# One transfer per block of x for both partition halves, and v's second weight split placed ahead of a normalisation

## The chip, the core and the metric

The kernel runs on one core of a Trainium2 chip. A core has a TensorE (PE in the profile, with its weight loads shown as PEld), a VectorE (DVE), a ScalarE (ACT), a GpSimd (POOL) and a SyncE (SP). SP and POOL issue the transfers that this text is about, each from its own instruction queue; 16 DMA engines carry them out. The metric is the device time of one execution in microseconds (us), and the number compared is the median of several runs. The profile is one further execution, with its own time.

## The reference

```python
xn = _layernorm(x, axis=-1)                    # x: 1 x 2048 x 576
s  = attention(xn)                             # 32 heads of 18 columns, wqkv, softmax, wo
g  = _silu(((xn @ w_gate) * (xn @ w_up)) @ w_down)   # 4608 columns in between
return x + s * g
```

Everything is float32. The kernel keeps that precision by writing each operand as a high part in the matmul's own format and a low rest, and by adding the products high by high, low by high and high by low.

## The kernel before

**Setting up (the first 195 us).** The 2048 rows of x are taken in four chunks of 512 (`NCH`). Each chunk is normalised (`norm`), turned into columns by transposes (`to_columns`), and multiplied with the weights of q and k in nine blocks of 128 columns (`qk_block`). The results go to DRAM (`sqk`). The weights of v come in two halves: `v_fetch(h)` loads one, `v_split(h)` makes its high part on ACT (line 493) and its low part on POOL (line 494), five pieces each. `v_block` (line 502) multiplies a group of 128 rows with both halves, so the first `v_block`, right after chunk 1, needs `v_split(1)` done. The columns of chunks 1 to 3 go to DRAM too (`sx`, nine blocks for each chunk, by `x_store`).

**The main part (195 to about 2505 us).** TensorE is used as two halves of 64 rows each, r = 0 and r = 1. On the one half runs "up" of the gated unit, on the other "gate": both multiply with the same columns of x, so every block of x stands twice in the pair of tiles `xg`, in partitions 0 to 63 and again in 64 to 127. The loop over gated units goes chunk by chunk, 18 units in each (`units`, `NF2`). A unit has two pairs of 27 matmuls for each half (`gu_op`, line 753; three in a row use one block of x, blocks 0 to 8) and then its down product (`down_op`, line 804). Between these matmuls stand those of attention: scores for the row maximum (line 648), transposed scores for the softmax (line 700) and the product with v (line 711).

**How a new chunk of x comes in.** There are three changes of chunk. In a chunk's last unit, each half, when it has done its three matmuls with a block (`k % 3 == 2`), issues the transfer of that block of the next chunk into its own 64 partitions: r = 0 from SP's queue and r = 1 from POOL's (`x_block`, lines 461 to 468). Block 4 spans both tiles and takes two transfers. The waiting is done by the issuing queue: a transfer is held there until TensorE has read the old block.

**What sets the order.** The whole main part is an order written out before it runs: `order()` (line 1249) keeps a planner's clock for each half and each engine and picks the next instruction by due times. `there["x", c, b, r]` (lines 962 and 964) is the time at which the planner believes that a block has landed; a gated matmul of the new chunk is placed no earlier. `moved` (line 1017) is the planner's clock of the SP queue. Each engine then runs its own list strictly in that order.

Of the kernel before, what the change touches and what calls it, by code (L numbers as in the profile page):

```python
# [20 lines left out]
FT = mybir.dt.float32  # L21
# [20 lines left out]
def kernel(  # L42
# [10 lines left out]
    nc = tc.nc  # L53
# [20 lines left out]
    sx = dram.tile([NCH, 9, 64, 2, 512], FT, name="sx")  # L74
# [9 lines left out]
    def bank(tag, bufs, k=None):  # L84
        if tag == "g":
            if k is None:
                k = turns[0] = (turns[0] + 1) % 4
            return psum.tile([128, 512], FT, name="pg", tag=f"g{k}", bufs=1)
        return psum.tile([128, 512], FT, name="p" + tag, tag=tag, bufs=bufs)
# [78 lines left out]
    clk, free, split_at = [0.0, 0.0], {"DVE": 0.0, "ACT": 0.0, "POOL": 0.0}, {}  # L168
# [7 lines left out]
    def engine(eng, start, length):  # L176
        start = max(free[eng], start)
        free[eng] = start + max(length - HIDDEN[eng], 0.03)
        return start + length
# [150 lines left out]
    def load_x(c):  # L330
        xin[c] = ep.tile([128, 4, D], FT, name="xin", bufs=2)
        for t in range(4):
            nc.sync.dma_start(xin[c][:, t, :], x2[c * 512 + t * 128:c * 512 + t * 128 + 128, :])
# [28 lines left out]
    def norm(c, ts=range(4)):  # L362
        for t in ts:
            norm_stats(c, t)
        for t in ts:
            norm_apply(c, t)
# [73 lines left out]
    def qk_block(b, c):  # L440
        w, ninth = (t[:, b % 2] for t in wq[b // 2])
        p = bank("a" if nqk[0] % 2 else "b", 2)
        nqk[0] += 1
        for n, (a, e) in enumerate(QK_PAIRS):
            nc.tensor.matmul(p, w[:, a, :] if a < 9 else ninth, xcs[c][:, e, :], start=n == 0,  # L445
                             stop=n == len(QK_PAIRS) - 1)
        hl = pp.tile([128, 2, 512], FR, name="hl", bufs=3)
        nc.scalar.activation(hl[:, 0, :], p, AF.Copy)
        nc.vector.tensor_tensor(hl[:, 1, :], p, hl[:, 0, :].bitcast(FT), op=OP.subtract)
        g0 = blocks[b]  # L450
        for kind in range(2):
            lo, hi = max(g0, kind * D), min(g0 + 128, (kind + 1) * D)
            if lo < hi:
                dst = sqk[kind, :, lo - kind * D:hi - kind * D, c * 512:(c + 1) * 512]
                nc.sync.dma_start(dst.rearrange("h r s -> r h s"), hl[lo - g0:hi - g0].bitcast(FT))


    def x_part(b, part):
        return divmod(2 * b + part, 9)

    def x_block(c, b, r):
        queue = nc.gpsimd if r else nc.sync
        if b == 4:
            for part in range(2):
                queue.dma_start(xg[part][r:r + 64, 8 - 8 * part, :].bitcast(FT), sx[c, b, :, part, :])
        else:
            i, k = x_part(b, 0)
            queue.dma_start(xg[i][r:r + 64, k:k + 2, :].bitcast(FT), sx[c, b])

    vbox, vrows, vturn = {}, [], [0]  # L470

    def more_rows(pool, n):
        for _ in range(n):
            vrows.append(pool.tile([128, H, DH + 1], FT, name=f"vo{len(vrows)}"))
            nc.gpsimd.memset(vrows[-1], 1.0)
# [10 lines left out]
    def v_split(h):  # L486
        if h == 0:
            vbox["w"] = vp.tile([128, 10, D], FR, name="wv")
            more_rows(vp, 3)
        raw, wv = vbox["raw"], vbox["w"]  # L490
        cs = slice(h * HALF, (h + 1) * HALF)
        for k, d, lo in ((0, 0, 4), (1, 1, 5), (2, 2, 6), (3, 3, 7), (4, 8, 9)):
            nc.scalar.activation(wv[:, d, cs], raw[:, k, :], AF.Copy)
            nc.gpsimd.tensor_tensor(wv[:, lo, cs], raw[:, k, :], wv[:, d, cs].bitcast(FT),
                                    op=OP.subtract)
# [16 lines left out]
    def w_now(i):  # L512
        wq[i], todo = w_split(raws[i], 1 if i == 4 else 2, ep if i == 2 else pp if i == 4 else None)
        for f, a in todo:
            f(*a)

    def w_fetch(i):
        raws[i] = w_load([(wqkv, b) for b in blocks[2 * i:2 * i + 2]])
# [27 lines left out]
    for c in range(NCH):  # L546
        if c + 2 < NCH:
            load_x(c + 2)
        for b in range(3):
            qk_block(b, c)  # L550
            if c == 0 and b == 0:
                w_now(2)
        if c + 1 < NCH:
            to_columns(c + 1)
        for b in range(3, 6):
            qk_block(b, c)
            if b < 5 and c + 2 < NCH:
                norm(c + 2, (0, 1) if b == 3 else (2, 3))
            if c in (1, 2):
                x_store(c, range(3 * (b - 3), 3 * (b - 2)))  # L560
            if c < 2 and b == 3:
                v_split(c)
            if c == 0 and b == 5:
                v_fetch(1)
            if c == NCH - 1 and b == 3:
                w_now(3)
        if c == 1:
            w_fetch(3)
            for t in range(4):
                v_block(t)  # L570
            w_fetch(4)
        if c == 2:
            w_now(4)
# [21 lines left out]
    for t in range(8, NT):  # L595
# [4 lines left out]
        if t == 11:  # L600
            xg = [xcp.tile([128, 9, 512], FR, name="xc")]
# [28 lines left out]
    with ExitStack() as mid:  # L630
# [115 lines left out]
        def gu_start(r, n):  # L746
            ready(gdone, n)
            return bank("g", 1, slots[r, "g"])
# [45 lines left out]
        def alone(u, n):  # L794
            return u == len(units) - 1 and n == 7
# [148 lines left out]
            wos[1] = wpool.tile([128, 2, D], FR, name="wos2", tag="wgu", bufs=2)  # L944
            nc.sync.dma_start(wos[1].bitcast(FT), swo[:, 8:10, :])

        passed, xdone = {}, []

        def stream(r, kind):

            def glu(n):
                c, q = units[n // 2]
                box = []
                for k in range(len(TERMS)):
                    def work(k=k):
                        if k == 0:
                            box.append(gu_start(r, n))
                        gu_op(r, n, box[0], k)
                        if q == NF2 - 1 and n % 2 and k % 3 == 2 and c < NCH - 1:
                            x_block(c + 1, k // 3, 64 * r)  # L960
                            if r:
                                there["x", c + 1, k // 3, r] = engine("POOL", clk[r] + 0.5, 0.75 + 0.6 * (k == 14)) + 3.0
                            else:
                                there["x", c + 1, k // 3, r] = moved(clk[r] + 0.5, 0.285)
                        if n == 2 * len(units) - 1 and k == 13:
                            xdone.append(r)
                            if len(xdone) == 2:
                                wo_fetch()
                        if k == len(TERMS) - 1:
                            highs.append((gate_end if r else up_end)(n, box[0]))  # L970
                    end = (("DVE", 0.685) if r else ("ACT", 0.595)) if k == len(TERMS) - 1 else None
                    yield 0.231, k == 0, work, end, ("g", n, k), len(TERMS)

            def down(u, n):
                own = alone(u, n)
                key = u, n, r * own
                s, i = divmod(n, 2)
                for k in range(len(DTERMS)):
                    def work(k=k):
                        if (own or r == 0) and k == 0:  # L980
                            passed[key] = down_start(r, u)
                        down_op(r, u, s, i, passed[key], k, {"POOL": nc.gpsimd, "ACT": nc.scalar, "DVE": nc.vector}[soonest()])
                        if (own or r) and k == len(DTERMS) - 1:
                            acts.append(by_act(u, i, clk[r] + 0.33))
                            down_end(u, s, i, passed.pop(key), acts[-1])
                    end = None
                    if (own or r) and k == len(DTERMS) - 1:
                        end = (None, 0.0)
                    yield 0.132, (own or r == 0) and k == 0, work, end, ("d", u, 6 * n + k), len(DTERMS)

            if kind == "g":
                for n in range(2 * len(units)):
                    yield from glu(n)
            else:
                for u in range(len(units)):
                    for n in range(8):
                        yield from down(u, n)
# [19 lines left out]
        def moved(start, size):  # L1017

            queue[0] = max(queue[0], start) + size / 0.24
            return queue[0] + 2.0  # L1020

        due, jobs, rows_done = [], [], {}
        there, queue = {}, [0.0]
        na = nb = 0
        part_work = len(units) * (2 * 27 * 0.231 + 4 * 12 * 0.132)
        part = part_work + (TOTAL + N + LEAD) * 0.231
# [417 lines left out]
```

## Time and profile before

| what | value |
|---|---|
| median of 3 runs | 2612.92 us (2612.11 to 2613.13) |
| the profiled execution, its own time | 2611.95 us |
| its span, first to last instruction | 2610.2 us |
| granted TensorE clock, mean | 1.000 |
| moved by the DMA engines | 434.34 MB, 166 GB/s over the span |
| transfers of x blocks in the main part | 24 of 256 KB and 6 of 128 KB from SP, the same from POOL |

The page has the busy time of each engine, the span in 40 slices, the DMA queues, the chain of work that ended last, the costliest groups of instructions and the DMA issues. Beside it stand answers of the trace: who waited for whom, instructions in order of time, and busy time by stage. In rows of instructions, "out<-in" names the tiles, then come partitions x elements, the count, and in brackets the idle time before with what ended it. `xc` is the name under which the tiles `xg` stand in the profile, since they take that pool's buffers.

### The profile page before, as it was taken

To read this page: it belongs to the slowest core of one execution; us is meant where nothing else is said; L and a number is where in the kernel's file an instruction comes from. 1 tells how busy PE (TensorE), PEld (TensorE's weight loads), DVE (VectorE), ACT (ScalarE), POOL (GpSimd) and SP (SyncE) were. 2 spreads that over 40 slices of the span, in tenths; PEclk is the share of its full clock that TensorE was granted. 3 is DMA by queue.
4 is the path that set the end of the run, shared out by engine and by line. 5 is a ranking of instruction groups with operands and counts; after the bars stand their busy time and mean duration, and the time that the engine had idled before them with its cause. 6 is when DMAs were issued, how large, how long until landed. Compare 5 with 4: busy or idle time off the path is not lost.

```text
span 2610.2 us, 59616 instructions
## 1 busy us (share of the span) xinstructions
PE 2595.7 (99%) x24504; PEld 2130.0 (82%) x24504; DVE 1795.3 (69%) x2985; ACT 1564.0 (60%) x3119; POOL 691.1 (26%) x731
## 2 busy tenths in 40 slices
PE   8999999999999999999999999999999999999999
PEld 7899878777878877887778888778788778777789
DVE  7208677677777877777777777777777777777436
ACT  4223667676766666666656666666666566666742
POOL 3114545343421222222121222112121222112115
PEclk9999999999999999999999999999999999999999
DMA  7799767667573534554463445344564444343356
GB/s 239 236 293 260 205 189 207 177 194 198 173 189 114 167 129 144 175 159 149 144 174 124 139 158 151 121 135 137 146 174 130 142 142 148 128 136 109 110 200 214
DMA packets 206928, 434.34 MB, mean 166 GB/s; under 512 B 82976, under 2 KB 132800, under 8 KB 176448
## 3 DMA queue, kind: packets, MB, share of 16 engines
q1 hardware_dynamic: 202288, 415.48, 52.6%
q0 software_dynamic: 4368, 15.04, 2.0%
q8 instruction: 193, 3.16, 0.5%
q14 instruction: 79, 0.65, 0.1%
HBM read 314.64 MB, written 110.56 MB: 163 GB/s over the span
## 4 chain that ended last, share of the span: by engine, by line
PE 96%; DMA 2%; DVE 1%; SPq 1%; ACT 0%; issue 0%; POOL 0%; ACTq 0%; DVEq 0%
PE pg L753 35%; PE pg L711 17%; PE pg L804 16%; PE pa L648 11%; PE pb L700 9%; PE pg L1396 2%; PE pg L502 1%; PE pb L445 1%; PE pa L445 1%; DMA sqk<-hl 1%; SPq L534 1%; DVE st L342 0%; DMA draw<-in_B_w_down_dram 0%; DMA sv<-vo 0%; PE pb L1373 0%; DVE mx L650 0%
## 5 line engine op out<-in xcount | busy, mean ns | idle before, releaser
L650 DVE TENSOR_REDUCE mx<-pa 128x1 f32<-128x512 f32 x2016 | 1345.6, 686 | 318.8 <-PE pa L648 182.7
L702 ACT ACTIVATE pt<-pb 128x512 f32<-128x512 f32 x2004 | 1148.7, 601 | 525.8 <-PE pb L700 384.8
L753 PE MATMUL pg<-xc,wgu 64*128 64x512 f32 x7776 | 1391.9, 391 | 0.1
L753 PEld LDWEIGHTS pg<-xc,wgu 64*128 64x128 f32 x7776 | 1053.7, 186 | 55.9 <-issue 0.8
L804 PE MATMUL pg<-wd,hs 64*128 64x288 f32 x6816 | 827.0, 293 | 0.7 <-DVE acc L867 0.7
L804 PEld LDWEIGHTS pg<-wd,hs 64*128 64x128 f32 x6816 | 773.9, 185 | 11.8 <-DVE acc L867 0.9
L648 PE MATMUL pa<-whole,turning 54*128 54x512 f32 x1999 | 783.5, 398 | 0.0
L700 PE MATMUL pb<-whole,turning 56*128 56x512 f32 x1987 | 778.5, 399 | 0.0
L711 PE MATMUL pg<-pt,vt 128*32 128x512 f32 x4096 | 459.3, 594 | 0.9 <-DVE acc L867 0.8
L784 POOL TENSOR_TENSOR hs<-us,hs 128x512 fp32r<-128x512 f32 x144 | 186.2, 1293 | 894.7 <-ACT hs L771 718.0
L648 PEld LDWEIGHTS pa<-whole,turning 54*128 54x128 f32 x1999 | 363.8, 184 | 71.8 <-issue 60.5
L700 PEld LDWEIGHTS pb<-whole,turning 56*128 56x128 f32 x1987 | 361.3, 185 | 7.0
L831 POOL TENSOR_TENSOR acc<-acc,st 128x288 f32<-128x288 f32 x288 | 231.7, 808 | 505.2 <-ACT st L861 289.4
L711 PEld LDWEIGHTS pg<-pt,vt 128*32 128x32 f32 x4096 | 123.3, 110 | 277.3 <-issue 269.0
L717 DVE TENSOR_TENSOR oc<-oc,pg 128x512 f32<-128x512 f32 x64 | 44.0, 687 | 287.9 <-PE pg L711 287.9
L254 POOL TENSOR_TENSOR wgu<-wraw,wgu 128x384 fp32r<-128x384 f32 x108 | 108.0, 1016 | 194.8 <-ACT wgu L253 108.8
L861 ACT ACTIVATE st<-pg 128x288 f32<-128x288 f32 x288 | 118.8, 413 | 31.3 <-PE pg L804 21.3
L867 DVE TENSOR_TENSOR acc<-acc,pg 128x288 f32<-128x288 f32 x257 | 114.6, 448 | 29.5 <-PE pg L804 24.1
L766 DVE TENSOR_TENSOR us<-pg,us 128x512 f32<-128x512 f32 x144 | 98.5, 684 | 31.4 <-PE pg L753 26.3
L759 ACT ACTIVATE us<-pg 128x512 f32<-128x512 f32 x144 | 86.2, 599 | 38.9 <-PE pg L753 31.3
L771 ACT ACTIVATE hs<-us 128x512 fp32r<-128x512 f32 x144 | 90.8, 631 | 10.6 <-DVE us L766 10.3
L715 ACT ACTIVATE oc<-pg 128x512 f32<-128x512 f32 x32 | 19.1, 598 | 127.6 <-PE pg L711 127.6
(147 smaller groups left out, 1290.7 us busy)
## 6 DMA issues: line engine op xcount, KB each, us to landing
wgu<-swg SPq DMA_DIRECT2D x102, 1152.0 KB
wd<-swd SPq DMA_DIRECT2D x50, 1152.0 KB
swg<-wgu SPq DMA_DIRECT2D x36, 1152.0 KB
whole<-sqk SPq DMA_DIRECT2D x192, 144.0 KB
turning<-sqk SPq DMA_DIRECT2D x384, 72.0 KB
swd<-wd SPq DMA_DIRECT2D x18, 1152.0 KB
sqk<-hl SPq DMA_DIRECT2D x32, 512.0 KB
wraw<-in_B_w_up_dram SPq DMA_DIRECT2D x36, 288.0 KB
```

What stands on the lines that cost most here:

```text
L254: nc.gpsimd.tensor_tensor(w[:, 9 + b:12 + b, :], raw[:, b:b + 3, :], w[:, b:b + 3, :].bitcast(FT), op=OP.subtract)
L648: nc.tensor.matmul(p, q[rows, t * 128:(t + 1) * 128], k[rows, c * 512:(c + 1) * 512], start=True, stop=True)
L650: nc.vector.tensor_reduce(mx[h][:, t, c:c + 1], p, axis=AX.X, op=OP.max)
L700: nc.tensor.matmul(p, k[rows, t * 128:(t + 1) * 128], q[rows, c * 512:(c + 1) * 512], start=True, stop=True)
L702: nc.scalar.activation(pt[t, c // 2][:, c % 2, :], p, AF.Exp, scale=scale)
L711: nc.tensor.matmul(p[32 * c:32 * c + 32, :], vt[h // 2][:, t, 6 * (h % 2):6 * (h % 2) + 32], pt[t, c // 2][:, c % 2, :], start=t == ts[0], ...
L753: nc.tensor.matmul(ps, gw[n][half[r], a, :], xg[i][half[r], e, :], start=k == 0, stop=k == len(TERMS) - 1)
L784: nc.gpsimd.tensor_tensor(hj[:, 1, :], h32, hj[:, 0, :].bitcast(FT), op=OP.subtract)
L804: op = nc.tensor.matmul(ps[:, 0:HALF], hs[u][half[r], j, a, s * 128:(s + 1) * 128], dw[u][half[r], j, e, i * HALF:(i + 1) * HALF], start=( ...
L831: nc.gpsimd.tensor_tensor(a, a, st, op=OP.add)
L861: nc.scalar.activation(st, ps[:, 0:HALF], AF.Copy)
L867: nc.vector.tensor_tensor(a, a, ps[:, 0:HALF], op=OP.add)
```

## The change

A block of the next chunk of x is brought by one transfer into all 128 partitions. Its destination is the 128 partitions of the tile; its source is the block in DRAM (64 rows) with a leading dimension of 2 and step 0, so the block is read twice. It is issued when the second of the two halves has done its matmuls with the old block (`xhalf` remembers the first). Even blocks go by SP's queue and odd ones by POOL's. The planner's landing times for a block are rewritten to match. Apart from that, `v_split(1)` is called ahead of `norm(3, (0, 1))` rather than behind it.

```diff
-    def x_block(c, b, r):
-        queue = nc.gpsimd if r else nc.sync
+    def both_halves(tile, src):
+        return tile.bitcast(FT), src.unsqueeze(0).broadcast_to([2] + list(src.shape))
+
+    def x_block(c, b):
+        queue = nc.gpsimd if b % 2 else nc.sync
         if b == 4:
             for part in range(2):
-                queue.dma_start(xg[part][r:r + 64, 8 - 8 * part, :].bitcast(FT), sx[c, b, :, part, :])
+                queue.dma_start(*both_halves(xg[part][:, 8 - 8 * part, :], sx[c, b, :, part, :]))
         else:
             i, k = x_part(b, 0)
-            queue.dma_start(xg[i][r:r + 64, k:k + 2, :].bitcast(FT), sx[c, b])
+            queue.dma_start(*both_halves(xg[i][:, k:k + 2, :], sx[c, b]))
...
             qk_block(b, c)
+            if c == 1 and b == 3:
+                v_split(c)
             if b < 5 and c + 2 < NCH:
                 norm(c + 2, (0, 1) if b == 3 else (2, 3))
...
-            if c < 2 and b == 3:
+            if c == 0 and b == 3:
                 v_split(c)
...
-        passed, xdone = {}, []
+        passed, xdone, xhalf = {}, [], set()
...
                         if q == NF2 - 1 and n % 2 and k % 3 == 2 and c < NCH - 1:
-                            x_block(c + 1, k // 3, 64 * r)
-                            if r:
-                                there["x", c + 1, k // 3, r] = engine("POOL", clk[r] + 0.5, 0.75 + 0.6 * (k == 14)) + 3.0
-                            else:
-                                there["x", c + 1, k // 3, r] = moved(clk[r] + 0.5, 0.285)
+                            b = k // 3
+                            if (c, b) in xhalf:
+                                x_block(c + 1, b)
+                                at = moved(clk[r] + 0.5, 0.45)
+                                if b % 2:
+                                    at = max(at, engine("POOL", clk[r] + 0.5, 0.75) + 2.0)
+                                there["x", c + 1, b, 0] = there["x", c + 1, b, 1] = at
+                            xhalf.add((c, b))
```

In the changed file lines behind 461 stand three to eight lower: the block's transfers are at 468 and 471 (465 and 468 before), the gated matmul at 758 (753), the down matmul at 809 (804), the scores at 653 and 705 (648 and 700).

SP's queue at the first change of chunk, before:

```order
L154 DMA draw<-in_B_w_down_dram 128x2x576
L736 DMA so<-ot 32x16x36 x4
L319 DMA turning<-sqk 18x1024 x3
L468 DMA xc<-sx 64x1024 x4
L465 DMA xc<-sx 64x512 x2
L468 DMA xc<-sx 64x1024 x4
L319 DMA turning<-sqk 18x1024 x3
L686 DMA whole_1154<-mr 1x16x128 x2
```

and in the change:

```order
L154 DMA draw<-in_B_w_down_dram 128x2x576
L741 DMA so<-ot 32x16x36 x4
L319 DMA turning<-sqk 18x1024 x3
L471 DMA xc<-sx 128x1x1024 x2
L468 DMA xc<-sx 128x1x512 x2
L471 DMA xc<-sx 128x1x1024 x2
L319 DMA turning<-sqk 18x1024 x3
L691 DMA whole_1154<-mr 1x16x128 x2
```

Ten transfers of 64 partitions became six of 128, of blocks 0, 2, 4 (in two), 6 and 8; their neighbours in the queue are the same. POOL's list at the same place, before:

```order
L292 TENSOR_TENSOR wd<-draw,wd 128x576 x2
L468 DMA xc<-sx 64x1024 x3
L784 TENSOR_TENSOR hs<-us,hs 128x512
L468 DMA xc<-sx 64x1024
L465 DMA xc<-sx 64x512 x2
L468 DMA xc<-sx 64x1024 x4
L784 TENSOR_TENSOR hs<-us,hs 128x512
```

and in the change:

```order
L292 TENSOR_TENSOR wd<-draw,wd 128x576 x2
L471 DMA xc<-sx 128x1x1024
L789 TENSOR_TENSOR hs<-us,hs 128x512
L471 DMA xc<-sx 128x1x1024 x3
L789 TENSOR_TENSOR hs<-us,hs 128x512
```

Ten became four, of blocks 1, 3, 5 and 7. TensorE's list is the same matmul for matmul until the third change of chunk. There the gated matmuls of the new chunk (line 753) stand behind most of the down matmuls before:

```order
L804 MATMUL pg<-wd,hs 128x288 x2
L753 MATMUL pg<-xc,wgu 128x512
L648 MATMUL pa<-whole_1153,turning 128x512
L804 MATMUL pg<-wd,hs 128x288 x10
L700 MATMUL pb<-whole_1154,turning 128x512
L804 MATMUL pg<-wd,hs 128x288
L648 MATMUL pa<-whole_1153,turning 128x512
L804 MATMUL pg<-wd,hs 128x288
L700 MATMUL pb<-whole_1154,turning 128x512
L804 MATMUL pg<-wd,hs 128x288 x13
```

and are mixed with them (as line 758, down matmuls as line 809) in the change, so that the new chunk begins right behind the old one's last matmul:

```order
L653 MATMUL pa<-whole_1153,turning 128x512
L809 MATMUL pg<-wd,hs 128x288 x2
L758 MATMUL pg<-xc,wgu 128x512
L809 MATMUL pg<-wd,hs 128x288 x2
L758 MATMUL pg<-xc,wgu 128x512
L809 MATMUL pg<-wd,hs 128x288
L758 MATMUL pg<-xc,wgu 128x512
L705 MATMUL pb<-whole_1154,turning 128x512
L758 MATMUL pg<-xc,wgu 128x512
L809 MATMUL pg<-wd,hs 128x288 x2
```

In setting up, ACT's list changes around the second v split (the piece of the difference; `rs` is the square root of a normalisation, `hl` the result of a `qk_block`):

```order
 L448 ACTIVATE hl<-pa 128x512
+L496 ACTIVATE wv<-wvraw 128x288 x5
 L344 ACTIVATE rs<-mv,eps 128x1 x2
-L493 ACTIVATE wv<-wvraw 128x288 x5
 L448 ACTIVATE hl<-pb 128x512
```

The five pieces of the split moved ahead of two square roots of the normalisation of chunk 3.

## The prediction

> **What bounds the kernel now.** I read the page first (busy time and the chain that ended last), then TensorE's waits, then the 80 us around each change of chunk by stage.
>
> ```profile
> span 2610.2 us, 59616 instructions
> PE 96%; DMA 2%; DVE 1%; SPq 1%; ACT 0%; issue 0%; POOL 0%; ACTq 0%; DVEq 0%
> PE pg L502 <- POOL wv L494: 1.0, 3, 0.4
> 700.00:780.00 80.00, 79.16 (x781) 64.37 (x775) 58.27 (x96) 51.36 (x100) 25.95 (x29) 1.00 0.68 178
> 1290.00:1370.00 80.00, 79.37 (x807) 63.04 (x808) 59.44 (x99) 47.95 (x94) 20.29 (x26) 1.00 0.61 169
> 1885.00:1965.00 80.00, 80.00 (x794) 63.99 (x792) 57.11 (x96) 50.55 (x101) 22.24 (x30) 1.00 0.55 151
> ```
>
> 96% of the chain is TensorE's own work. The third row says that it waited for the low part of v's weights three times, 1.0 us in all. In the last three rows the first number behind the comma is TensorE's busy time: at the changes of chunk it stands still for 0.84, 0.63 and 0.00 us of 80. So x comes in behind other work, and the change can hardly gain: 0.84 + 0.63 + 1.0 = 2.5 us if every one of these stops went away. It can lose much more, if a block lands late: each engine runs a fixed list, and TensorE's next matmul with a missing block holds all behind it.
>
> **How many DMA engines a transfer uses** decides that, and the trace answers it indirectly.
>
> ```profile
> DMA packets 206928, 434.34 MB, mean 166 GB/s; under 512 B 82976, under 2 KB 132800, under 8 KB 176448
> wgu<-swg SPq DMA_DIRECT2D x102, 1152.0 KB
> ...
> whole<-sqk SPq DMA_DIRECT2D x192, 144.0 KB
> turning<-sqk SPq DMA_DIRECT2D x384, 72.0 KB
> ...
> vt<-sv SPq DMA_DIRECT2D x16, 304.0 KB
> ...
> so<-ot SPq DMA_DIRECT2D x64, 72.0 KB
> ...
> turning<-mr SPq DMA_DIRECT2D x2, 8.0 KB
> ```
>
> The issues of this list (first and last row quoted) add up to 1285 on SP and 57 on POOL, 1342 transfers. Two kinds move pieces under 512 bytes: `so` in pieces of 36 floats, 64 x 72 KB / 144 B = 32,768 packets, and `vt` in pieces of 38 floats, 16 x 304 KB / 152 B = 32,768. That leaves 82,976 - 65,536 = 17,440 small packets that are nobody's data: the engines' reports of completion. If each transfer made 16 there would be 1342 x 16 = 21,472. The difference is 4,032 = 576 x 7, and 576 is the number of transfers of `whole` and `turning` from `sqk`, the ones of 18 rows. So these report from 9 engines and all others from 16: the number of engines is a divisor of the outermost count, 9 of 18, 16 of 64 or 128. The arithmetic comes out to the packet.
>
> The new transfer has an outermost count of 128 at its destination and of 2 at its source (the leading step-0 dimension). No transfer of this trace has two different counts. If the smaller side sets the number, as it must if each engine is to get whole shares of both sides, it runs on 2 engines.
>
> [...]
>
> **The change part by part.**
>
> *Issues.* SP loses 12 (30 to 18 in the three changes) and POOL 18 (30 to 12). Neither queue is on the chain, so this is worth 0; the cover is TensorE's work.
>
> *Bytes.* A block of 512 KB in place of two of 256 KB: the same 4.6 MB for each change of chunk.
>
> *Time of a block.* On 16 engines 512 KB take 2.1 us at the rate of the row below; that is one end, and gives no wait (below). On 2 engines each carries 262,144 B. What one engine does is the moved rate over the busy share and 16:
>
> ```profile
> 730.00:740.00 10.00, 9.95 (x108) 9.68 (x104) 8.88 (x15) 7.55 (x16) 6.99 (x11) 1.00 1.04 247
> 2480.00:2500.00 20.00, 20.00 (x184) 14.43 (x178) 3.43 (x6) 15.33 (x32) 2.57 (x2) 1.00 0.47 178
> DMA to landing us min/median/max: 2.4/2.9/7.2
> ```
>
> With all engines loaded (first row, share 1.04) it is 247 / 1.04 / 16 = 14.8 GB/s; half loaded (second row) 178 / 0.47 / 16 = 23.7. With two engines at work and the rest nearly idle I take 23.7: 11.07 us for a block, 17.7 at 14.8. The third row, of the 288 KB stores of `sg`, gives 2.4 us from issue to landing where a transfer is small; I add it once.
>
> [...]
>
> *The queues.* SP's five blocks (0, 2, 4, 6, 8) follow each other on the same two engines if those are always the same; POOL's four I take to fall on others. So SP's ninth block lands 5 x 11.07 + 2.4 = 57.8 us after block 0 is released. When the release comes, and when TensorE needs block 8, is in these rows:
>
> ```profile
> 729.03 0.67 POOL L468 DMA_DIRECT2D xc<-sx  x1 [10.59 <-PE pg L753]
> 749.29 0.40 PE L753 MATMUL pg<-xc,wgu 64*128 64x512 f32 x1
> 756.74 0.63 PE L753 MATMUL pg<-xc,wgu 64*128 64x512 f32 x3
> ...
> 1313.92 0.53 POOL L468 DMA_DIRECT2D xc<-sx  x1 [8.91 <-PE pa L648]
> 1341.58 0.63 PE L753 MATMUL pg<-xc,wgu 64*128 64x512 f32 x3
> ...
> 1906.20 0.53 POOL L468 DMA_DIRECT2D xc<-sx  x1 [8.54 <-PE pa L648]
> 1919.84 0.51 POOL L468 DMA_DIRECT2D xc<-sx  x1 [0.80 <-PE pa L648]
> ...
> 757.44 1.08 PE L753 MATMUL pg<-xc,wgu 64*128 64x512 f32 x7
> 738.63 0.79 PE L804 MATMUL pg<-wd,hs 64*128 64x288 f32 x8
> ```
>
> POOL's first issue is the moment when the second half lets go of block 0. TensorE begins the new chunk at 749.29 and comes to the first half's 25th matmul, the first with block 8, at 757.0 (the second of the row 756.74). First change: 729.0 + 57.8 = 786.8, against 757.0: 29.8 us late. Second: 1313.9 + 57.8 = 1371.7, against 1341.6: 30.1. At the third the order is new: by its list 129 matmuls lie between the last release (1919.8) and the first use of block 8, 47 gated, 27 scores and 55 down. The last two rows give their pitch, (1.08 - 0.39) / 6 = 0.115 us and (0.79 - 0.29) / 7 = 0.071, so 74 x 0.115 + 55 x 0.071 = 12.4 us, need at 1932.2; landing at 1906.2 + 57.8 = 1964.0: 31.8. The waits for blocks 2, 4 and 6 lie inside these. Sum 91.7 us.
>
> POOL's block 7 is issued about 738 and lands 13.5 us later, at 752, before it is needed at about 756: nothing.
>
> *What is queued behind.* On SP the `turning` loads and the rows of maxima `mr` of the next head; on 9 or 16 engines they too pass the two loaded ones, behind block 8. Their share there is 24 KB and less, about 1 us, and TensorE resumes with gated matmuls first. I count 0; without that cover it is 1 us a change.
>
> *The v split.* The rows are from ACT's timeline and, the last two, from the chain of waits.
>
> ```profile
> 53.61 0.60 ACT L448 ACTIVATE hl<-pa 128x512 fp32r<-128x512 f32 x1 [3.73 <-DMA sqk<-hl]
> 55.94 0.29 ACT L344 ACTIVATE rs<-mv,eps 128x1 f32<-128x1 f32 x1 [1.73 <-DVE mv L343]
> 57.06 1.76 ACT wv L493 x5
> 59.32 2.31 POOL wv L494 x3
> ```
>
> The split can start at 54.2 instead of 57.06, POOL ends 2.8 us sooner, and the 1.0 us of TensorE's waits goes. What comes later is the normalisation of chunk 3, by up to 1.8 us, the split's length; its transposes stand at 82.7 us, 20 us of matmuls away. So -1.0 us; between 0 and -1.0.
>
> *Sum.* 2610.2 + 91.7 - 1.0 = 2700.9 us of span. The profiled execution took 1.75 us more than its span (2611.95), and the median of the runs is 1.0 above it: 2703.6, rounded to **2704 us**.
>
> **Rivals.**
>
> *Sixteen engines* (the destination's 128 sets the number). A block takes 2.1 us, lands as early as today, and only the v split counts: 2612.9 - 1.0 = 2612 us, not slower. The point from which it decides: on k engines a block takes 22.1 / k us, and block 8 is in time while 5 x 22.1 / k + 2.4 is under 28 us, so from 5 engines on. For it: that `dma_start` is given 128 partitions. Against it: the 9 engines of the 18-row transfers.
>
> *Two loaded engines.* If an engine does 14.8 GB/s here as at 730 to 740 us, five blocks take 88.4 + 2.4 = 90.8 us; waits 62.8 + 63.1 + 64.8 = 190.7; 2803 us. Against it: the other 14 are nearly idle.
>
> *One pair for both queues.* If POOL's blocks fall on SP's two engines, nine blocks take 99.6 + 2.4 = 102.0 us: 74.0 + 74.3 + 76.0 = 224.3, 2836 us. The trace does not tell which engines POOL's would get; single meetings of the pairs lie between.
>
> *Faster.* All the stops named, 2.5 us, are less than 0.2% (5.2 us), so only an unforeseen gain of the new order would do it.
>
> **How the numbers follow.** Two engines at about 24 GB/s 0.70, two loaded 0.13, one pair 0.04, sixteen 0.11, faster 0.02. About 0.2% is what a measurement of this kernel tells from no change: faster 0.02; same 0.09, most of the sixteen; slower 0.89, with 0.02 for a small loss at the third change, where the new order leaves block 0 only some 13 us. The low end of the range takes an engine a third faster than the best row, as window means hold small packets too: 31.6 GB/s, 8.3 us a block, waits of 15.9 + 16.2 + 18.0 = 50 us, 2662, rounded out to 2655. The high end is the loaded case with some meeting of the pairs, 2820. Left out are 0.04 + 0.13 at the sides and about 0.03 of tails.
>
> **What would show it.** Right: TensorE idle some 30 us behind each change of chunk, waiting for `xc<-sx` in line 758, in steps of about 11 us, POOL's blocks not waited for; a DMA share near 2/16 in these stretches; the small packets, 17,440 - 60 x 16 + 18 x 2 + 12 x 2 = 16,540, or 16,708 if POOL's transfers report from all 16 engines whatever they use, against 16,960 on sixteen engines. The v split ending 2.8 us sooner. Wrong: no wait of line 758 for x, and 2612 us. A wait of POOL's blocks first would mean the one pair.

## The result and the profile after

The changed kernel takes 2729.88 us (median of 5 runs, 2729.32 to 2730.61) against 2612.45 us (median of 5, 2611.33 to 2613.13) for the one before: a ratio of 1.045, 95% interval 1.0435 to 1.0466. The profiled execution took 2729.88 us too, with a span of 2728.1 us. The prediction was 2704 us in a range from 2655 to 2820.

From the page of the changed kernel:

```profile
span 2728.1 us, 59552 instructions
PEclk9999999999969999999979999999969999999999
DMA packets 217140, 434.38 MB, mean 159 GB/s; under 512 B 92996, under 2 KB 142820, under 8 KB 186660
PE 92%; DMA 7%; DVE 0%; SPq 0%; issue 0%; ACT 0%
L758 PE MATMUL pg<-xc,wgu 64*128 64x512 f32 x7776 | 1422.6, 396 | 85.7 <-DMA xc<-sx 85.7
```

The chain that ended last holds 7% DMA (2% before), and the costliest group, the gated matmuls, now has 85.7 us of idle time in front of it, all ended by the transfers of x. Between the two profiles TensorE's busy time grows too, by 33.7 us (2595.7 to 2629.4), since it works between these waits at a granted clock of 0.50, where a matmul of 0.40 us lasts 0.79 (rows below). The row of the granted clock has three dips, one at each change of chunk. The bytes are the same to 0.04 MB, but there are 10,020 more small packets.

Where the loss falls is read from the same matmuls in both traces. From the timelines of TensorE, products with v around the first and after the second change, first before and then after (start, duration, engine and line):

```profile
719.34 4.50 PE L711 MATMUL pg<-pt,vt 128*32 128x512 f32 x40
813.86 4.50 PE L711 MATMUL pg<-pt,vt 128*32 128x512 f32 x40
1441.31 4.50 PE L711 MATMUL pg<-pt,vt 128*32 128x512 f32 x40
```

```profile
717.64 4.50 PE L716 MATMUL pg<-pt,vt 128*32 128x512 f32 x40
853.21 4.50 PE L716 MATMUL pg<-pt,vt 128*32 128x512 f32 x40
1514.34 4.50 PE L716 MATMUL pg<-pt,vt 128*32 128x512 f32 x40
```

Ahead of the first change the changed kernel is 1.70 us early: the split of v's weights. Behind the first change it is 39.35 us late, behind the second 73.03 us, at the end of the span 117.9. So the three changes cost 41.1, 33.7 and 44.9 us, where the last figure takes in all that follows the third change.

The changed kernel's timeline of TensorE at the first change, only the rows that waited for x (in brackets the idle time; the first wait is ended by POOL's block 1, all others by blocks of SP):

```profile
755.61 0.79 PE L758 MATMUL pg<-xc,wgu 64*128 64x512 f32 x1 [6.88 <-DMA xc<-sx]
761.69 0.79 PE L758 MATMUL pg<-xc,wgu 64*128 64x512 f32 x1 [4.02 <-DMA xc<-sx]
767.12 0.50 PE L758 MATMUL pg<-xc,wgu 64*128 64x512 f32 x2 [1.29 <-DMA xc<-sx]
772.62 0.80 PE L758 MATMUL pg<-xc,wgu 64*128 64x512 f32 x2 [4.53 <-DMA xc<-sx]
783.27 0.79 PE L758 MATMUL pg<-xc,wgu 64*128 64x512 f32 x1 [7.72 <-DMA xc<-sx]
793.39 0.80 PE L758 MATMUL pg<-xc,wgu 64*128 64x512 f32 x2 [6.34 <-DMA xc<-sx]
```

The last three starts, for SP's blocks 4, 6 and 8, are 10 to 11 us apart: one block on two engines. SP's queue at the same place (start, length of the issue, count), and the windows around the last wait (busy times, then granted clock, DMA share and GB/s):

```profile
727.02 2.39 SPq L471 DMA_DIRECT2D xc<-sx  x2
730.53 27.82 SPq L468 DMA_DIRECT2D xc<-sx  x2
758.44 10.67 SPq L471 DMA_DIRECT2D xc<-sx  x2
769.16 11.00 SPq L319 DMA_DIRECT2D turning<-sqk  x3
```

```profile
790.00:793.00 3.00, 0.00 (x0) 0.00 (x0) 0.00 (x0) 0.00 (x0) 0.00 (x0) 0.50 0.13 52
793.00:796.00 3.00, 2.61 (x12) 2.13 (x14) 0.69 (x1) 1.09 (x2) 0.00 (x0) 0.50 0.26 93
796.00:800.00 4.00, 4.00 (x22) 3.10 (x22) 2.36 (x4) 1.49 (x4) 0.00 (x0) 0.54 0.16 35
800.00:804.00 4.00, 4.00 (x37) 3.64 (x37) 2.72 (x5) 2.95 (x6) 1.29 (x1) 1.00 0.81 319
```

In the first window nothing runs but x: a share of 0.13 is 2 of 16 engines, at 52 / 0.13 / 16 = 25 GB/s each. Behind the wait TensorE works, but at half its clock until 800 us.

From the first of SP's issues to the matmul that block 8 releases, the three streams take 66.4 us (727.0 to 793.4), 58.7 and 66.3; the prediction had 57.8 for each.

### The profile page after: what moved, and what is told of

Read it like the earlier page. It is cut to its first block, busy times and chain, and to the rows that moved or that the text cites. A ratio compares the mean times of both kernels' runs of the same rounds, so it can differ in the third digit from the quotient of the medians.

```text
span 2728.1 us, 59552 instructions
## 1 busy us (share of the span) xinstructions
PE 2629.4 (96%) x24504; PEld 2146.1 (79%) x24504; DVE 1798.5 (66%) x2988; ACT 1565.5 (57%) x3116; POOL 683.0 (25%) x710
## 2 busy tenths in 40 slices
DMA packets 217140, 434.38 MB, mean 159 GB/s; under 512 B 92996, under 2 KB 142820, under 8 KB 186660
## 4 chain that ended last, share of the span: by engine, by line
PE 92%; DMA 7%; DVE 0%; SPq 0%; issue 0%; ACT 0%
PE pg L758 33%; PE pg L716 16%; PE pg L809 15%; PE pa L653 10%; PE pb L705 8%; DMA xc<-sx 7%; PE pg L1404 2%; PE pb L445 2%; PE pa L445 2%; PE pg L505 2%; DMA draw<-in_B_w_down_dram 0%; SPq L537 0%; PE pb L1381 0%; PE pg L385 0%; PE pa L705 0%; PE pb L653 0%
## 5 line engine op out<-in xcount | busy, mean ns | idle before, releaser
L758 PE MATMUL pg<-xc,wgu 64*128 64x512 f32 x7776 | 1422.6, 396 | 85.7 <-DMA xc<-sx 85.7
L758 PEld LDWEIGHTS pg<-xc,wgu 64*128 64x128 f32 x7776 | 1064.9, 188 | 155.0 <-DMA xc<-sx 89.0
L809 PE MATMUL pg<-wd,hs 64*128 64x288 f32 x6816 | 840.2, 294 | 0.7 <-DVE acc L872 0.7
L809 PEld LDWEIGHTS pg<-wd,hs 64*128 64x128 f32 x6816 | 786.1, 187 | 12.0 <-DVE acc L872 0.9
L705 PE MATMUL pb<-whole,turning 56*128 56x512 f32 x1995 | 787.9, 402 | 0.0
```

Source lines behind the costliest of these rows:

```text
L705: nc.tensor.matmul(p, k[rows, t * 128:(t + 1) * 128], q[rows, c * 512:(c + 1) * 512], start=True, stop=True)
L758: nc.tensor.matmul(ps, gw[n][half[r], a, :], xg[i][half[r], e, :], start=k == 0, stop=k == len(TERMS) - 1)
L809: op = nc.tensor.matmul(ps[:, 0:HALF], hs[u][half[r], j, a, s * 128:(s + 1) * 128], dw[u][half[r], j, e, i * HALF:(i + 1) * HALF], start=( ...
```

## The experiments

All were run against the kernel before on the same chip (medians 2611.6 to 2612.1 us). Diffs are against the changed kernel unless said otherwise.

**The v split alone** (the kernel before, with only the move of `v_split(1)`):

```diff
+            if c == 1 and b == 3:
+                v_split(c)
...
-            if c < 2 and b == 3:
+            if c == 0 and b == 3:
```

> The kernel before with the second v split moved alone; x comes in as before. Theory A (the cost is that a block's transfer with an outermost count of 2 runs on 2 DMA engines): 2612.45 - 1.74 = 2610.7 us, TensorE's 1.0 us of waits for wv gone, no wait for x. Theory B (the cost is the later issue, the new queues and the new order): the same, 2610.7. A loss here would mean that part of the 117 us is the split's.

2610.53 us, ratio 0.9995 (0.9986 to 1.0004); span 2608.5, 1.7 us under that of before. This half of the change does what was expected, and is too small for the runs to tell from nothing.

**Two transfers of 64 partitions, at the change's place and from its queues:**

```diff
-            queue.dma_start(*both_halves(xg[i][:, k:k + 2, :], sx[c, b]))
+            for r in (0, 64):
+                queue.dma_start(xg[i][r:r + 64, k:k + 2, :].bitcast(FT), sx[c, b])
```

> The change, but each block by two transfers of 64 partitions, both issued where the change issues its one, even blocks on SP and odd ones on POOL; issue time, queues, planner and the order of TensorE as in the change. Theory A: all transfers on 16 engines, no wait for x above 2 us in all, 2611 us (2608 to 2615). Theory B: still near 2730 us. Theory C (reading the same rows twice through a step of 0 is slow in itself): 2611 us.

2611.95 us, ratio 0.9999 (0.999 to 1.0007), no wait for x. Waiting for the second half, the even blocks on SP and the odd ones on POOL, and the new order of TensorE's list cost at most the 1.4 us that the v split gave: the loss is in the form of the transfer.

**One transfer from 128 neighbouring rows:**

```diff
+        rows = sx[c].rearrange("b p j s -> (b p) j s")[64 * min(b, 7):64 * min(b, 7) + 128]
...
-            queue.dma_start(*both_halves(xg[i][:, k:k + 2, :], sx[c, b]))
+            queue.dma_start(xg[i][:, k:k + 2, :].bitcast(FT), rows)
```

> The change, but the source of a transfer is 128 neighbouring rows of sx in place of 64 rows twice: the same bytes, one transfer, the same queue and place, outermost count 128 on both sides. The second half gets the rows of another block, so the gated product is another one. Theory A: 16 engines, 2611 us (2608 to 2615). Theory B: near 2730 us. Theory C: 2611 us.

2611.75 us, ratio 1.0 (0.999 to 1.0009). One transfer of 128 partitions is not the trouble either.

**Two groups of 64 rows with a gap between them**, so an outermost count of 2 with no step of 0 and nothing read twice:

```diff
+        two = sx[c, min(b, 6):min(b, 6) + 3:2]
...
-            queue.dma_start(*both_halves(xg[i][:, k:k + 2, :], sx[c, b]))
+            queue.dma_start(xg[i][:, k:k + 2, :].bitcast(FT), two)
```

> As with 128 rows, but the source is two groups of 64 rows with a gap between them: outermost count 2 again, and no step of 0, nothing is read twice. The second half gets the rows of another block, so the gated product is another one. Theory A: 2 engines, 2730 us (2720 to 2740). Theory C: 2611 us. Theory B: near 2730 us, which the two runs before tell from A.

2730.23 us, ratio 1.0454 (1.0439 to 1.0468). Its page has the changed kernel's numbers to the packet:

```profile
DMA packets 217140, 434.38 MB, mean 159 GB/s; under 512 B 92996, under 2 KB 142820, under 8 KB 186660
```

The whole loss is there without a broadcast. Apart from which rows are read, only the outermost count of the source distinguishes this run from the one before it; the runs with 4 and 8 groups below have gaps too and lose less, so the gap alone is not the cause.

**Only SP's even blocks by the new transfer**, POOL's odd ones as two halves:

```diff
+        if b % 2 == 0:
...
+                queue.dma_start(*both_halves(xg[i][:, k:k + 2, :], sx[c, b]))
+            return
...
+            for r in (0, 64):
+                queue.dma_start(xg[i][r:r + 64, k:k + 2, :].bitcast(FT), sx[c, b])
```

> Only SP's even blocks by one broadcast transfer; POOL's odd blocks by two of 64 partitions. Theory A: SP's five blocks follow each other on two engines at 10.5 us each and set the end; POOL's packets no longer meet them except with a sixteenth of each transfer. About 8 us less than the change at the first and third change of chunk, 2 less at the second: 2712 us (2700 to 2722); waits of line 758 for x about 70 us. If POOL's transfers made most of the loss: under 2660.

2730.86 us, ratio 1.0457 (1.0441 to 1.0472): a miss by 19 us, and SP's five blocks alone cost all of it. From the chain of waits of this run:

```profile
730.48 60.15 DMA xc<-sx x2
1353.43 61.66 DMA xc<-sx x2
1985.51 60.53 DMA xc<-sx x2
```

From SP's first issues (726.97, 1349.95 and 1982.29 us) the streams take 63.7, 65.1 and 63.8 us, alike at all three changes. Overlooked was that POOL's halves, if they run on all 16 engines, use SP's two as well. The traces don't name a packet's engine, so this is an estimate: four blocks of 512 KB leave 131 KB on each engine, half of what one confined block leaves there, so half of 11.07 us: 57.8 + 5.5 = 63.3 us.

**Only POOL's odd blocks by the new transfer** (`b % 2 == 1` in the same place):

> Only POOL's odd blocks by one broadcast transfer; SP's even ones by two of 64 partitions. Theory A with POOL's engines handed out in turn, a new pair for each transfer: blocks land some 13 to 18 us after their issue, side by side, about when they are needed; waits for x under 10 us in all, 2612 us (2609 to 2622). If POOL's four blocks follow each other on one pair: the last lands 4 x 10.5 + 2.4 = 44 us after the first, waits of about 15 us a change, 2655 us.

2649.96 us, ratio 1.0149 (1.0132 to 1.0166): near the higher of the two values, but not for the reason given with it. From its chain of waits:

```profile
728.33 25.75 DMA xc<-sx
1321.09 28.32 DMA xc<-sx
1923.53 26.80 DMA xc<-sx
```

One wait at each change, for block 1, the first that POOL issues (at 728.33 us in the first). It needs 26 to 28 us to land, not the 13.5 that the prediction gave a block of POOL's. The four blocks don't follow each other: at the first change they land at 754.1, 754.4, 755.0 and 755.5 us, so the time came out near 2655 us by luck. The parts don't add up (119 us and 38 us alone, 117 together); both delays lie in the same stretch.

**The pairs shifted by one tiny transfer from POOL's queue at the start:**

```diff
+    one = consts.tile([128, 4], FT, name="one")
+    nc.gpsimd.dma_start(one, x2[0:64, 0:4].unsqueeze(0).broadcast_to([2, 64, 4]))
```

> The change, with one tiny broadcast transfer (2 x 64 rows of 16 bytes, unused) issued from POOL at the start. If POOL's engines are handed out in turn, two for each broadcast, the change's first block at the first and third change of chunk falls on SP's pair (4 blocks x 2 engines x 2 changes = 16) and not at the second; shifted by one pair, it no longer does, and only the last block of the second does. Landing of POOL's blocks at the first and third then 16 us at least, as at the second now (27.3 and 25.6 now); 8 us less at each of these, some 5 more at the second: 2720 us (2714 to 2726). If the slow landings have another reason: 2730 us.

2719.76 us, ratio 1.0414 (1.0399 to 1.043): 10 us faster than the change, as expected, by a transfer that nobody uses. Time from issue to landing of POOL's four blocks at the three changes, first in the changed kernel, then in this run:

```profile
DMA to landing us min/median/max: 27.3/35.2/42.8
DMA to landing us min/median/max: 16.2/21.8/25.8
DMA to landing us min/median/max: 25.6/33.7/35.9
```

```profile
DMA to landing us min/median/max: 17.1/25.1/32.6
DMA to landing us min/median/max: 16.4/21.8/35.9
DMA to landing us min/median/max: 17.0/25.0/27.0
```

SP's streams take 56.1, 68.5 and 57.6 us here, where they took 66.4, 58.7 and 66.3: the long ones moved from the first and third change to the second. A fixed pair for SP and pairs in turn for POOL would give that. Four blocks of two engines at each change would step through eight of the 16 and meet SP's pair at every second change, and one more transfer would move the meeting to the other one. This is inferred from the times of the two runs; no trace says on which engine a packet ran.

The kept traces hold every DMA packet with its queue, and they show when SP's stream is slowed. Counted in steps of 3 us, SP's queue moves 128 to 152 KB (in packets of 2 and 4 KB) in each step from 1358 to 1394 us, in the changed kernel's second change. In its first change it moves only 64 to 76 KB from 735 to 753 us, and in its third 72 to 80 KB from 1987 to 2005 us: about half; that a block of POOL's has the other half of the pair is the inference above. In the shifted run this happens at the second change alone, with 48 to 92 KB from 1372 to 1390 us.

**Only block 0 by the new transfer** (`b == 0` in the same place):

> Only block 0 by one broadcast transfer, all others by two of 64 partitions. Theory A: one such block lands 13.5 us after its issue, ahead of its need at the first two changes and about with it at the third; 2612 us (2609 to 2616), so that the loss comes from five such blocks in one queue and not from one. If a broadcast transfer holds its queue or the chip in another way: 10 us or more for each change, over 2640.

2637.44 us, ratio 1.0099 (1.0084 to 1.0114): a miss by 25 us. From its chain of waits, and from SP's queue:

```profile
726.80 24.71 DMA xc<-sx
```

```profile
732.13 21.80 SPq L481 DMA_DIRECT2D xc<-sx  x4
```

A single confined block needs 24 to 25 us at each change, and SP's next four issues were held for 21.8 us. At 25 GB/s its 262 KB would take 10.5 us on each of two engines. But here these engines would also have their sixteenth of all the other blocks, in a stretch in which the DMA share with two halves is 1.04 (730 to 740 us): at the 14.8 GB/s that the prediction quotes for 730 to 740 us, 262 KB take 17.7 us, and the shares of other transfers in between would make up the rest (an estimate; no run separates them). The reports of completion, of which each transfer from POOL leaves 16, fit that: for the one issued at 728.0 us, fourteen come by 733.5 us and the last two at 737.8 and 738.5.

**Four groups of 32 rows, and eight of 16,** in place of the two of 64 with a gap:

```diff
+        rows = sx[c, min(b, 5):min(b, 5) + 4, 0:32]
...
-            queue.dma_start(*both_halves(xg[i][:, k:k + 2, :], sx[c, b]))
+            queue.dma_start(xg[i][:, k:k + 2, :].bitcast(FT), rows)
```

(with eight, `sx[c, min(b, 1):min(b, 1) + 8, 0:16]`)

> The blocks hold other rows of x (four groups of 32 rows from four neighbouring blocks), so the output is not the reference's; bytes, order and queues are those of the change. The source has an outermost count of 4. Theory (the outermost count is the number of engines, and TensorE waits as long as SP's stream of five blocks is late): each of 4 engines carries half of what it did with 2, so SP's stream of about 59 to 66 us falls to some 30 to 35 us, against the 28 us in which it is needed: 2 to 7 us late at each change. About 2625 us (2617 to 2640). Small packets by the same count of empty ones: 65,536 + 17,440 - 960 + 18 x 4 + 12 x (16 + 12 x 32) = 86,888. Rival (only a count of 2 is special, or any gap in the source costs): 2611, or again 2730.

> As the run with 4, but with eight groups of 16 rows: an outermost count of 8. Theory: 8 engines, SP's stream lands within some 20 us and is in time at all three changes, as the prediction has it from 5 engines on: 2611 us (within 2), no wait of the gated matmuls for x. Small packets 65,536 + 17,440 - 960 + 18 x 8 + 12 x (16 + 8 x 16) = 83,888. Rival (the loss goes with 1 over the count and has no threshold, 118 us x 2/8): 2640.

2667.53 us, ratio 1.0212 (1.0197 to 1.0227), and 2628.83 us, ratio 1.0061 (1.0044 to 1.0078). From their pages:

```profile
DMA packets 211032, 434.35 MB, mean 163 GB/s; under 512 B 86888, under 2 KB 136712, under 8 KB 180552
```

```profile
DMA packets 208032, 434.34 MB, mean 165 GB/s; under 512 B 83888, under 2 KB 133712, under 8 KB 177552
```

The small packets are 86,888 and 83,888, the expected numbers to the packet, which were worked out with 4 and 8 engines. The times are misses by 43 and 18 us. Against the 2610.5 us of the v split alone the loss is 119, 57, 18 and 1 us at counts of 2, 4, 8 and 128 (the last is the run of 128 neighbouring rows). It halves from 2 to 4, but there is no point at 5 engines where it ends. Neither of the rivals stated beforehand fits (2611 or 2730 us at 4, 2640 at 8). From the chains of waits of the two runs, at the first change:

```profile
729.02 40.89 DMA xc<-sx x2
```

```profile
733.92 27.42 DMA xc<-sx
```

SP's stream takes 42.1 us on 4 engines and 35.0 on 8, where the expectation had 30 to 35 and 20. Windows of 10 us at this place, for counts of 4, 8 and 128:

```profile
730.00:740.00 10.00, 9.34 (x104) 9.08 (x102) 9.20 (x16) 7.19 (x14) 4.45 (x5) 1.00 0.68 149
```

```profile
730.00:740.00 10.00, 9.18 (x103) 8.08 (x104) 9.11 (x16) 6.10 (x12) 2.68 (x4) 1.00 0.95 152
```

```profile
730.00:740.00 10.00, 9.19 (x105) 8.68 (x105) 9.21 (x17) 6.62 (x14) 3.20 (x5) 1.00 0.86 302
```

149 / 0.68 / 16 = 13.7 GB/s for each busy engine, 10.0 and 21.9. With 8 the engines are nearly always busy (0.95) and with 4 two thirds of the time (0.68), yet together they move half of what the whole-width transfers do. The expectation used 23.7 GB/s throughout. The small packets described below are not the reason: in this window they take 5% of the busy time at a count of 4 and 1% at 8. The 4 KB packets themselves last longer, those of POOL's queue 286 and 413 ns (median) against 159 ns with whole-width transfers; why, the runs don't say.

None of these versions is measurably faster than the kernel before.

## Why the prediction was right and where it was off

*Two engines.* Right, and shown from several sides: the last window before block 8 has a DMA share of 0.13, 2 of 16; two halves (2611.95 us) and 128 neighbouring rows (2611.75) lose nothing; a count of 2 without a broadcast (2730.23) loses everything; 4 and 8 lie between.

*23.7 GB/s for an engine.* Right for the case it was used for. Where, as inferred, no block of POOL's meets SP's pair, the stream takes 58.7 us in the changed kernel and 56.1 and 57.6 in the shifted one, against 57.8 predicted. (The 2.4 us in that sum is the least of stores of 288 KB and not of a small transfer, as the prediction has it.)

*POOL's blocks on other engines, landing after 13.5 us.* This step failed. They landed 16.2 to 42.8 us after issue, and at the first and third change SP's stream was 66.4 and 66.3 us long, by the inference from the shifted run because one of them fell on SP's pair. That adds 8.6 us and 8.5 us, with the second change's 0.9 us 18.0 in all. The prediction named "single meetings of the pairs" as a possibility and put them in the upper end of the range, not in the sum. That POOL's pairs come in turn rests on that run alone, where one tiny transfer turned streams of 66.4, 58.7 and 66.3 us into 56.1, 68.5 and 57.6.

What the step left out is that a landing of POOL's needs 16 reports: at the first change fourteen of block 1's come by 731.1 us and the last two at 755.0 and 755.6, and the matmul that waits for it begins at 755.61. At the second change block 1, issued at 1354.3 us, has twelve reports by 1356.9, two more at 1367.9 and 1368.1, which is 13.8 us after the issue and near the 13.5 predicted, and the last two only at 1370.5. POOL's transfers also leave packets of 4 bytes beyond their reports (last section). From 756 to 776 us, when all of POOL's data is in, 374 packets of 4 bytes from its queue pass and 368 data packets of SP's, so about one for one; I take the late ones to be on SP's pair. So POOL's blocks were waited for after all: block 1 ends the first wait of the first change (6.88 us) and one of the third (4.90 us). The prediction had taken a wait for POOL's blocks first as the sign of one pair for both queues; here, by the same inference, it was the meeting of one block with SP's pair. These waits lie ahead of SP's last block and don't set the end.

*The clock.* Not counted at all. Of 41.1, 33.7 and 44.9 us, the streams as measured explain 29.8 + 8.6, 30.1 + 0.9 and 31.8 + 8.5; there remain 2.7, 2.7 and 4.6 us, 10.0 in all. Behind the last wait of each change TensorE works almost without a pause, but at half its clock. For the second and third change these windows begin with it (third number from the end: the granted clock):

```profile
1411.00:1414.00 3.00, 2.20 (x11) 0.90 (x15) 0.00 (x0) 0.00 (x0) 0.00 (x0) 0.50 0.12 46
2045.00:2050.00 5.00, 4.68 (x35) 4.54 (x37) 1.57 (x3) 1.64 (x3) 0.00 (x0) 0.61 0.18 59
```

By the clock's record in the trace it is 1.00 again at 799.7, 1417.5 and 2048.9 us, 6.3, 5.7 and 3.6 us after the last waits. Half of that is lost work, 3.2, 2.9 and 1.8 us, so 7.8 of the 10.0. Of the rest 1.7 us may be the new order of TensorE's list, by which the span of the run with two halves (2610.2) exceeds that of the v split alone (2608.5). This was read from traces; no run holds the clock apart. By the same record the clock went to 0.50 eight times at the three changes, each time within a wait for `xc`, and these waits are 2.94 to 7.90 us long.

*The v split.* The right sign, mis-sized: 1.0 us predicted, 1.70 measured. From the timelines of ACT and POOL after:

```profile
53.62 1.77 ACT L496 ACTIVATE wv<-wvraw 128x288 fp32r<-128x288 f32 x5
```

```profile
54.13 4.09 POOL L497 TENSOR_TENSOR wv<-wvraw,wv 128x288 fp32r<-128x288 f32 x5 [15.72 <-ACT wv L496]
```

POOL ends at 58.2 us rather than 61.6, 3.4 us sooner and not 2.8, and the waits for `wv` are gone. What they cost was mis-sized. From the timeline of TensorE before:

```profile
60.17 0.40 PE L502 MATMUL pg<-wv,xcx 128*128 128x288 f32 x1 [0.30 <-POOL wv L494]
60.92 0.40 PE L502 MATMUL pg<-wv,xcx 128*128 128x288 f32 x1 [0.35 <-POOL wv L494]
61.67 4.50 PE L502 MATMUL pg<-wv,xcx 128*128 128x288 f32 x32 [0.35 <-POOL wv L494]
```

The prediction added the idle times in brackets, 1.0 us. But the matmuls begin 0.75 us apart, and 0.13 us apart where nothing is waited for, since each then begins before the one ahead of it has ended. So a wait costs about 0.6 us, and three make 1.8.

*What is queued behind.* Counted as 0, and rightly: all 17 waits of TensorE for transfers at the changes are waits for `xc`, although SP's queue was held up, where two issues of block 4 took 27.8 us and three of `turning` 11.0.

*The sum.* 2700.9 us of span + 18.0 (longer streams) + 10.0 (remainder) - 0.7 (v split) = 2728.2, measured 2728.1. This closes by construction, as the 10.0 is what the streams leave over; with 7.8 for the clock and 1.7 for the new order, each read by itself, it is 2727.7. So the time lay in the range because the price of the main mechanism was right, and 26 us above the forecast because the meetings and the clock were not in the sum. The runs lie 1.8 us above it, where I had added 2.75.

*The small packets.* Predicted 16,540 or 16,708 that are nobody's data; there are 92,996 - 65,536 = 27,460. SP's new transfers do leave two reports each (block 8's at the first change at 792.7 and 793.4 us), but each of POOL's leaves 912 packets, which is 16 + 14 x 64: 17,440 - 960 + 18 x 2 + 12 x 912 = 27,460. The runs with one queue's blocks confined confirm the division between the queues. SP's even blocks first, then POOL's odd ones:

```profile
DMA packets 206580, 434.33 MB, mean 159 GB/s; under 512 B 82436, under 2 KB 132260, under 8 KB 176100
DMA packets 217680, 434.38 MB, mean 164 GB/s; under 512 B 93536, under 2 KB 143360, under 8 KB 187200
```

65,536 + 17,440 - 960 + 18 x 2 + 24 x 16 = 82,436 and 65,536 + 17,440 - 960 + 36 x 16 + 12 x 912 = 93,536, both to the packet.

*The rivals.* Sixteen engines is ruled out by the wait, and two fully loaded engines and one pair for both by the streams, which are 56 to 69 us long and not 91 or 102. The point that the first rival gave, in time "from 5 engines on", was wrong: 8 engines still lose 18 us.

## What to carry to other kernels

Before merging transfers look at the outermost count of the source too, not only at the partitions of the destination: a leading dimension of 2, by broadcast or by stride, confined 512 KB to two of 16 engines (a DMA share of 0.13), and two transfers of half the size were as good as one of full width (2611.95 and 2611.75 us). Price a confined transfer with everything else that is on its engines, since one such block alone took 24 us in a busy stretch against 11 by the rate of a lone engine. And add to each series of long waits the slow clock behind it, here 2 to 3 us by the granted clock.

## What the runs showed of the hardware that was not expected

- A transfer from POOL's queue with a count of k leaves small packets beyond its 16 reports: 12 transfers left 12 x 14 x 64 at a count of 2, 12 x 12 x 32 at 4 and 12 x 8 x 16 at 8, to the packet. They are packets of 4 bytes, the "empty" ones of the expectations. In the shifted run the tiny transfer left 14 packets of 256 bytes instead. These numbers fit 4 bytes for each row of a working engine on each engine without data (64 x 4 B = 256 B); this is an inference from the counts. SP's transfers leave none: the 82,436 of the run with SP's even blocks has two reports for each of them and nothing more.
- POOL's confined blocks land 16 to 43 us after issue, with the last of the 16 reports far behind most of the others (block 1 of the second change: twelve by 1356.9 us, the last two at 1370.5). By my inference these last two come from engines that SP keeps busy and that carry none of the block's data.
- SP's queue is held at the changes: 27.8 us for two issues in the changed kernel, 21.8 for four in the run with one block.
- With counts of 4 and 8 a busy engine moved 13.7 and 10.0 GB/s, against 21.9 with whole-width transfers at the same place and 25 for two engines alone.
